# Fewer and wider warm-up matmuls, one matrix loaded in four parts, and two pairs of steps in another order, in a fused attention and mixture kernel

## The chip, the cores and the metric

The kernel runs on one core of one Trainium2 chip. The metric is the device time of one execution in microseconds (us); lower is better. Five engines work side by side, each through its own list of instructions: TensorE (PE in the profile; its weight loads are PEld), VectorE (DVE), ScalarE (ACT), GpSimd (POOL) and SyncE (SP). POOL and SP mostly issue DMA transfers here.

## What is computed

Two stages, the second fed by the first (from the reference, shortened):

```python
# q, k, v: 4 batches x 8 heads x 768 x 64;  sort_net: 4 x 8 x 8 x 8
for _ in range(5):
    P = exp(P - max(P));  P = P / sum(P, -1);  P = P / sum(P, -2)
k_sorted, v_sorted = P @ blocks_of(k), P @ blocks_of(v)     # 8 blocks of 96 rows are mixed
attn = softmax(q_blk @ k_sorted_blk.T / 8)                  # inside each block
x = (attn @ v_sorted_blk), heads side by side               # 3072 x 512
out = sum over 4 experts of p[:, e] * (relu(x @ w1[e]) @ w2[e])   # w1: 512 x 1024, w2: 1024 x 512
```

## The kernel before

The whole order of work is written out by hand; no scheduler moves anything. It falls into three stretches.

**The head (0 to about 28 us).** DVE and ACT run the five normalisation rounds on a 32 x 64 tile (lines 283 to 299), a strict chain of small operations. PE has nothing real to do yet and runs dummy matmuls: `warm(84)` at line 280 and `warm(30)` at line 288, each a 128x128 stationary tile with 128 moving columns. Between the two it transposes the first half of batch 0's queries (`h_q`, line 264). When the weights of the mixing are ready, `r_half(0)` (line 314) spreads half of them into PSUM, `build_PI0` makes mixing matrices, and `mix_half` and `mixed` (lines 485 and 503) mix batch 0's keys and values for four of the eight blocks: the product on PE, the evacuation from PSUM on ACT or DVE. `h_s` (scores and exponential), `h_w` (values transposed), `h_a` (attention times values), `h_x` (result transposed) follow for each quad of heads, interleaved with `group0`, the first expert's first layer (lines 1365 to 1417). Line 1370 spreads the other half of the weights (`r_half(1)`), after the first scores `h_s(0, 0)` and before the transposes of `h_w`; line 1372 copies all of them from PSUM to the tile `Rs`, on DVE. PSUM tiles come from two pools of two buffers each, `psM` and `psA`, handed out in turn, so a new tile waits until the last reader of the tile two before it is done. `mix_half("k", 1, 0, psm)` at line 1378 takes the buffer that line 1372 reads.

**The loads.** POOL issues the large loads in program order: queries, keys and values of batch 0, then `load_w1(0, 2)` (line 173), the first expert's first matrix in two parts of 256 rows each, and only then makes the masks (lines 175 to 204) and, at line 304, half of the spread weights (the other half is DVE's). Eight completion semaphores take turns, and a load waits until the load eight before it has landed. `group0` reads the matrix in the order: rows 0 to 255 with columns 0 to 511, rows 0 to 255 with columns 512 to 1023, then rows 256 to 511 in the same way.

**The middle (about 28 to 186 us) and the end.** The experts' products run chunk by chunk (`chunk`, line 809). Between two products stands a call of `slot()`, and a hand-written table, `PLANS`, says which attention step of the next batches runs in which slot: an entry `(c, n, f, b, pr)` runs step `f` for batch `b` and pair of heads `pr` in slot `n` of chunk `c`. `st_k` (line 392) mixes keys on PE and evacuates with four ACT copies (line 408); `st_v` (line 361) mixes values on PE, evacuates with one ACT copy (line 371) and, for every second pair, issues six DMAs on SP that move the values to `vs` (line 379); `st_s` is scores and exponential (line 425), `st_a` attention times values (lines 453, 434, 435). In slot 8 of batch 1's chunk 1 the second table, `PLAN_A`, also begins `input_sums`: an ACT multiplication (line 997) followed by a DMA that adds (line 998). After slot 9, `chunk` copies the product of bank A with ACT (line 856), and DVE adds bank B to that copy (line 857):

```python
            times(bankB, blk(1, 0), "b21", es)
            slot()
            nc.scalar.copy(p1[:], bankA)
            tt(oa1, bankB, p1[:], ALU.add)
            times(bankQ, sm(0), "t1", es)
            nc.scalar.copy(p5[:], bankQ)
            slot()
            ...
            times(bankA, sm(1), "t2", es, False)
```

Banks A and B are halves of one PSUM tile, and the product `t2` goes into bank A again. From 186 us on the remaining products run without attention steps.

Of the kernel before, what the change touches and what calls it, by code (L numbers as in the profile page):

```python
# [17 lines left out]
def kernel(  # L18
# [11 lines left out]
    nc = tc.nc  # L30
# [8 lines left out]
    P = 128  # L39
# [10 lines left out]
    KH = NFC // 2  # L50
# [16 lines left out]
    def psa(shape, dtype, name):  # L67
        state["n"] += 1
        return psA.tile(shape, dtype, tag="ps", name=name)
# [36 lines left out]
    def load_natural(b, nm, qd):  # L106
        src = {"k": k, "v": v}[nm]
        t = arena[:, ds(("k", "v").index(nm) * 2 * NW + qd * NW, NW)].rearrange("p (h r d) -> p h r d", h=4, r=R)
        natural[(b, nm, qd)] = t
        nc.gpsimd.dma_start(  # L110
            t.rearrange("p h r d -> p h (r d)"),
            src[b, ds(4 * qd, 4)].rearrange("h (p r) d -> p h (r d)", r=R),
        )
# [12 lines left out]
    w1sb, w2sb = [], []  # L126
# [4 lines left out]
    def load_w1(e, parts=1):  # L131
        n = NKC // parts
        for i in range(parts):
            nc.gpsimd.dma_start(
                w1sb[e][:, ds(i * n, n)], moe_w1[e].rearrange("(kc p) f -> p kc f", p=P)[:, ds(i * n, n)]
            )
# [8 lines left out]
    def load_half_queries(hf):  # L145
        for qd in range(2):
            nc.gpsimd.dma_start(
                q0[ds(64 * qd, 64), hf].rearrange("p h r d -> p h (r d)"), half_queries(qd, hf)
            )

    dummy = Hflat[:, ds(2 * NFC * 2 * P, P)]
# [18 lines left out]
    load_natural(0, "v", 0)  # L170
    load_natural(0, "k", 1)
    load_natural(0, "v", 1)
    load_w1(0, 2)

    eye16 = const.tile([P, CP], F16, name="eye16")
    maskk = const.tile([P, P], F16, name="maskk")
# [13 lines left out]
    kTs, ETs, vs0s, wide = [], [], [], []  # L190
# [38 lines left out]
    def spread_weights():  # L229

        nc.vector.tensor_reduce(p_den, p_in, AX.X, ALU.add)
        yield
        nc.vector.tensor_scalar(out=p_den, in0=p_den, scalar1=1e-9, scalar2=None, op0=ALU.add)
        yield
        nc.vector.reciprocal(p_den, p_den)
        yield
        nc.vector.tensor_tensor(
            p_out.rearrange("p e t -> p t e"), p_in, p_den.broadcast_to([P, NT, E]), ALU.mult
        )
        p_rows = p_dram.rearrange("e (p t) -> p e t", t=NT)  # L240
        nc.sync.dma_start(p_rows[0:S_P], p_out[0:S_P])
        nc.sync.dma_start(p_0, p_dram[0, 0:S].rearrange("(t p) -> t p", p=P))
        pbs[(0, 0)] = load_p(0, 0)
        nc.sync.dma_start(p_rows[S_P:P], p_out[S_P:P])
        yield
# [7 lines left out]
    qTs = {}  # L253
    q_ring = const.tile([P, 3, R, P], F16, name="q_ring")

    def warm(n):
        ps = psM.tile([P, 4, P], F32, tag="ps", name=f"ps_w_{state['n']}")
        state["n"] += 1
        for m in range(n):
            nc.tensor.matmul(ps[:, m % 4, :], dummy, dummy, start=True, stop=True)  # L260

    qT0 = [from_spare(2 * S).rearrange("p (s f r x) -> p s f r x", s=2, f=2, r=R) for _ in range(2)]

    def h_q(qd, hf, copy):

        ps = psa([P, 2, R, 64], F16, f"ps_q_{qd}_{hf}")
        rows = ds(64 * qd, 64)
        for sg in range(2):
            for r in range(R):
                for hh in range(2):  # L270
                    nc.tensor.transpose(
                        ps[ds(D * hh, D), sg, r, :], q0[rows, hf, 2 * sg + hh, r, :], ident[rows, rows]
                    )
        copy(qT0[qd][:, :, hf], ps[:])
# [2 lines left out]
    srow = const.tile([GH, NB, 1], F32, name="srow")  # L277
    scol = const.tile([GH, NB, 1], F32, name="scol")
    sn16 = const.tile([GH, NB, NB, CP], F16, name="sn16")
    warm(84)  # L280
    p_steps = spread_weights()
    nc.gpsimd.tensor_copy(ident6, ident[0:R, 0:R])
    for it in range(5):
        nc.scalar.activation(sn[:], sn[:], AF.Exp, bias=0.0, scale=1.0)
        if it == 4:
            for qd in range(2):
                h_q(qd, 0, nc.scalar.copy)
            warm(30)
        nc.vector.tensor_reduce(srow[:], sn[:], AX.X, ALU.add)
        nc.vector.reciprocal(srow[:], srow[:])  # L290
        nc.vector.tensor_tensor(sn[:], sn[:], srow[:].broadcast_to([GH, NB, NB]), ALU.mult)
        nc.vector.tensor_reduce(scol[:], sn[:].rearrange("p i j -> p j i"), AX.X, ALU.add)
        nc.vector.reciprocal(scol[:], scol[:])
        if it < 4:
            nc.vector.tensor_tensor(
                sn[:], sn[:],
                scol[:].rearrange("p j o -> p o j").broadcast_to([GH, NB, NB]),
                ALU.mult,
            )
            if it:  # L300
                next(p_steps)
# [10 lines left out]
    Rv = ps_R[:, :, 0:HB * GH].rearrange("p a (i g) -> p a i g", g=GH)  # L312

    def r_half(a):
        for i in range(HB):
            nc.tensor.matmul(
                Rv[:, a, i, :], sn16[:, a * HB + i, :, :].rearrange("g j c -> g (j c)"),
                ident[0:GH, 0:GH], start=True, stop=True,
            )
# [4 lines left out]
    Rs = const.tile([P, GH, NB], F16, name="Rs")  # L324
# [31 lines left out]
    vec, act = nc.vector.tensor_copy, nc.scalar.copy  # L356
# [128 lines left out]
    def mix_half(nm, qd, hf, pool, warm_up=0):  # L485

        ps = pool([P, 1024], F32, f"ps_m{nm}_{qd}_{hf}")
        keep_warm(ps[:, 0:P], warm_up)
        tails[(nm, qd, hf)] = ps[:, 2 * R * 64:1024].bitcast(F16).rearrange("p (n x) -> p n x", n=2)
        ps = ps[:, 0:2 * R * 64].rearrange("p (s r x) -> p s r x", s=2, r=R)  # L490
        for sg in range(2):
            for r in range(R):
                for hh in range(2):
                    h = 4 * qd + 2 * sg + hh
                    nc.tensor.matmul(  # L495
                        ps[ds(D * hh, D), sg, r, :],
                        head(0, nm, h)[:, r, :],
                        PI0[hf][:, h, :, :].rearrange("p i c -> p (i c)"),
                        start=True, stop=True,
                    )  # L500
        return ps

    def mixed(nm, qd, ps, i0, n, copy):

        dst = kTs[qd][:, 0:S] if nm == "k" else vT0[qd]
        copy(
            dst.rearrange("p (i x c) -> p x i c", i=HB, c=CP)[:, :, ds(i0, n)],
            ps.rearrange("p s r (i c) -> p (s r) i c", c=CP)[:, :, ds(i0, n)],
        )
# [30 lines left out]
    def h_s(qd, qq, ps=None):  # L540

        kT, ET = kTs[qd], ETs[2 * qd + qq % 2]
        if ps is None:
            ps = psa([P, 2, 512], F32, f"ps_s0_{qd}_{qq}")
        for n in range(4):
            for hh in range(2):
                sg, i = n // 2, 2 * (qq % 2) + n % 2

                m = BLK if 2 * i + sg == 3 else P
                nc.tensor.matmul(  # L550
                    ps[0:m, hh, ds(n * BLK, BLK)],
                    kT[ds(D * hh, D), ds((2 * i + sg) * BLK, m)],
                    qT0[qd][ds(D * hh, D), sg, qq // 2, :, ds((2 * (qq % 2) + n % 2) * CP, CP)],
                    start=True, stop=True,
                )
        nc.scalar.activation(
            ET[:, 0:S].rearrange("c (h x) -> c h x", h=2), ps[0:BLK, :, 0:HS],
            AF.Exp, bias=0.0, scale=SCALE,
        )
# [59 lines left out]
    def st_bk(b, qd):  # L619
# [24 lines left out]
            (0, 13, st_bv, 3, 1), (0, 14, st_a, 2, 3), (0, 14, st_x, 2, 2),  # L644
            (1, 0, st_k, 3, 0), (1, 1, st_v, 3, 1), (1, 1, st_x, 2, 3), (1, 1, st_q, 3, 2), (1, 2, st_s, 3, 0),
            (1, 3, st_k, 3, 1), (1, 4, st_v, 3, 2), (1, 4, st_q, 3, 3), (1, 4, st_bk, 3, 1), (1, 5, st_s, 3, 1),
            (1, 6, st_k, 3, 2), (1, 7, st_k, 3, 3), (1, 8, st_v, 3, 3), (1, 9, st_a, 3, 0), (1, 10, st_s, 3, 2),
            (1, 11, st_a, 3, 1), (1, 11, st_x, 3, 0), (1, 12, st_s, 3, 3), (1, 13, st_a, 3, 2), (1, 13, st_x, 3, 1),
            (1, 14, st_a, 3, 3), (2, 0, st_x, 3, 2), (2, 1, st_x, 3, 3),
        ],  # L650
# [715 lines left out]
    mixed("k", 0, mk0, 0, 2, act)  # L1366
    mv0 = mix_half("v", 0, 0, psa)
    mixed("v", 0, mv0, 0, 2, vec)
    h_s(0, 0)
    r_half(1)  # L1370
    mixed("k", 0, mk0, 2, 2, act)
    vec(Rs.rearrange("p g (a i) -> p a g i", a=2), Rv.rearrange("p a i g -> p a g i"))
    load_half_queries(1)
    load_w2(0, 2)
    build_PI0(nc.gpsimd, 1, 0, H, Rs[:, 0:H, HB:NB])
# [160 lines left out]
```

## Time and profile before

| | us |
|---|---|
| median of 3 runs | 359.47 |
| lowest and highest | 359.26, 360.56 |
| profiled execution, span from first to last instruction | 357.8 |
| PE busy in it | 351.6 (98%) |
| DVE, ACT, POOL busy | 276.2, 170.6, 133.6 |

The profile lists no other time for the profiled execution than its span, which lies 1.7 us under the median. How to read it: the page gives busy time by engine, the span in 40 slices, and the chain of work that ended last, followed back from the last instruction. Answers of the trace add, for any stretch, the instructions in order of time with the idle time ahead of each and what ended it (`[idle <-releaser]`), and the list of who waited for whom. By stretch, PE is busy for 9.96 of the first 12.00 us, 15.03 of the 16.00 us from 12 to 28, 131.99 of the 132.00 us from 28 to 160, 26.00 of the 26.00 us from 160 to 186, and 168.66 of the last 171.80 us. The granted clock reads 1.00 in all of these.

### The profile page before, as it was taken

The page shows a single profiled execution, that of the slowest core. Times are in us where ns is not written, and L with a number is a line of the kernel's source. Part 1 is how long each engine was busy: PE and PEld are TensorE (multiplying, and loading weights), DVE is VectorE, ACT ScalarE, POOL GpSimd, SP SyncE. Part 2 cuts the span into 40 slices and gives each one's busy share as a digit, 9 for nine tenths or more (in the row PEclk, how much of TensorE's full clock was granted, in tenths as well). Part 3 has the DMA queues.
Part 4 walks back from the last instruction along what each step waited for, and adds up shares of the span by engine and source line. Part 5 has one row for each costly group of instructions (what it writes and reads, how often), then busy time and mean ns, then how long its engine had stood idle before and what let it go on. Part 6 is the DMA issues. An engine that isn't in the chain of part 4 may idle for free.

```text
span 357.8 us, 9498 instructions
## 1 busy us (share of the span) xinstructions
PE 351.6 (98%) x3949; PEld 306.3 (86%) x3949; DVE 276.2 (77%) x552; ACT 170.6 (48%) x303; POOL 133.6 (37%) x149
## 2 busy tenths in 40 slices
PE   8899999999999999999999999999999999999996
PEld 8686867888888888888899988888888888888886
DVE  5754797869889587868978988896678886588963
ACT  2554240442434535367947258830288611688201
POOL 8864010375122222000535318840058800188400
PEclk9999999999999999999999999999999999999999
DMA  8999999999999999935996420005200015100011
GB/s 114 207 205 228 216 210 198 209 163 165 201 154 160 188 152 170 194 74 73 168 201 90 102 78 0 2 2 108 102 29 2 3 39 138 61 0 2 2 73 46
DMA packets 72022, 40.51 MB, mean 113 GB/s; under 512 B 40614, under 2 KB 66732, under 8 KB 71980
## 3 DMA queue, kind: packets, MB, share of 16 engines
q0 software_dynamic: 36576, 19.93, 41.9%
q1 hardware_dynamic: 35260, 19.92, 28.5%
q8 instruction: 31, 0.51, 0.6%
q14 instruction: 11, 0.09, 0.1%
q10 hardware_dynamic: 144, 0.07, 0.1%
HBM read 42.13 MB, written 6.34 MB: 135 GB/s over the span
## 4 chain that ended last, share of the span: by engine, by line
PE 95%; DVE 2%; ACT 1%; DMA 0%; issue 0%; DVEq 0%
PE ps_h L790 18%; PE ps_Q L1264 18%; PE ps_p L774 12%; PE ps_X L1121 10%; PE ps_Z L1121 7%; PE ps_Q L1121 7%; PE ps_Z L1264 6%; PE ps_h L679 3%; PE ps_o L714 3%; PE ps_p L830 3%; PE ps_a L453 2%; PE ps_s L418 2%; PE ps_k L399 1%; PE ps_v L365 1%; PE ps_a L567 1%; PE ps_mk L495 1%
## 5 line engine op out<-in xcount | busy, mean ns | idle before, releaser
L790 PE MATMUL ps_h<-xT,w 128*128 128x256 f16 x576 | 67.5, 273 | 0.0
L790 PEld LDWEIGHTS <-w 128*128 128x128 f16 x576 | 55.2, 98 | 7.2
L796 DVE SCALAR_TENSOR_TENSOR Hb<-ps_h,pb 128x1024 f16<-128x1024 f32 x34 | 41.5, 1223 | 17.2 <-PE ps_h L790 15.8
L1121 PEld LDWEIGHTS <-w 128*128 128x128 f16 x480 | 43.6, 98 | 4.8
L1134 POOL TENSOR_TENSOR arena<-tmp,pb 128x512 f16<-128x512 f32 x12 | 15.2, 1275 | 65.7 <-PE ps_Z L1121 49.8
L1264 PEld LDWEIGHTS <-Hb 128*128 128x128 f16 x320 | 31.1, 98 | 3.5
L1133 ACT ACTIVATE tmp<-tmp 128x512 f32<-128x512 f32 x46 | 29.0, 632 | 3.9 <-DVE tmp L1171 3.9
L1264 PEld LDWEIGHTS <-Sb 128*128 128x128 f16 x304 | 28.3, 98 | 3.0
L1121 PEld LDWEIGHTS <-arena 128*128 128x128 f16 x312 | 27.7, 98 | 2.9
L425 ACT ACTIVATE ET<-ps_s 96x768 f16<-96x768 f32 x24 | 18.0, 802 | 25.1 <-PE ps_s L418 24.8
L121 POOL DMA_DIRECT2D arena<-in_q_dram x24 | 19.9, 838 | 25.5 <-DMA q_ring<-arena 25.2
L408 ACT CAST kT<-ps_k 64x384 f16<-64x384 f32 x48 | 22.7, 473 | 13.3 <-PE ps_k L399 12.3
L1121 PE MATMUL ps_X<-ET,arena 128*128 128x256 f16 x168 | 25.2, 272 | 0.0
L1264 PE MATMUL ps_Q<-w,Hb 128*128 128x256 f16 x192 | 24.6, 273 | 0.0
L774 PEld LDWEIGHTS <-Hb 128*128 128x128 f16 x232 | 21.8, 98 | 3.0
L1127 DVE SCALAR_TENSOR_TENSOR Hb<-ps_X,pb 128x512 f16<-128x512 f32 x27 | 18.7, 691 | 7.0 <-PE ps_X L1121 7.0
L1141 ACT COPY ps_X<-ps_Z 128x512 f32<-128x512 f32 x27 | 15.4, 571 | 17.8 <-PE ps_Z L1121 17.8
L1121 PE MATMUL ps_Z<-xT,w 128*128 128x256 f16 (+1 forms) x176 | 22.5, 258 | 0.0
L760 DVE TENSOR_TENSOR Sb<-Hb 128x512 f16<-128x512 f16 x33 | 20.6, 647 | 0.0
L1148 ACT COPY tmp<-ps_X 128x512 f32<-128x512 f32 x26 | 15.2, 585 | 9.2 <-PE ps_X L1121 6.6
L1127 DVE SCALAR_TENSOR_TENSOR Hb<-ps_Z,pb 128x512 f16<-128x512 f32 x27 | 18.4, 682 | 1.3 <-PE ps_Z L1121 1.3
L1171 DVE TENSOR_TENSOR tmp<-ps_Q,tmp 128x512 f32<-128x512 f32 x26 | 17.8, 683 | 0.8 <-PE ps_Q L1121 0.8
(266 smaller groups left out, 741.6 us busy)
## 6 DMA issues: line engine op xcount, KB each, us to landing
w<-in_moe_w_dram POOLq DMA_DIRECT2D x6, 1024.0 KB, 27.9
pb<-p_dram SPq DMA_DIRECT2D x9, 512.0 KB, 7.0
arena<-in_k_dram POOLq DMA_DIRECT2D x8, 384.0 KB, 9.3
arena<-in_v_dram POOLq DMA_DIRECT2D x8, 384.0 KB, 7.5
vs<-arena SPq DMA_DIRECT2D x36, 66.0 KB, 4.9
arena<-in_q_dram POOLq DMA_DIRECT2D x24, 96.0 KB, 7.5
out_dram<-ob SPq DMA_DIRECT2D x9, 256.0 KB, 2.0
w<-in_moe_w_dram POOLq DMA_DIRECT2D x4, 512.0 KB, 12.5
```

What stands on the lines that cost most here:

```text
L121: nc.gpsimd.dma_start(t[:, h // 2, :, h % 2, :], q[b, h].rearrange("(t p) d -> p t d", p=P))
L408: nc.scalar.copy(kT[ds(D * hh, D), r], pk[ds(D * r, D), hh].rearrange("p a (i c) -> p a i c", c=CP),)
L425: nc.scalar.activation(ETs[2 * (pr % 2) + hh][:, 0:S].rearrange("c (a x) -> c a x", a=2), pss[hh][0:BLK, :, 0:HS], AF.Exp, bias=0.0, scale ...
L760: tt(sm[0], blk(0, 1), blk(1, 1), ALU.add)
L774: nc.tensor.matmul(ps, lhs(e, f), Ts[e][rhs][:, f, :], start=(first and e == es[0] and f == 0), stop=(done and e == es[-1] and f == KH - 1 ...
L790: nc.tensor.matmul(ps[:, f, :], w1sb[e][:, kc, ds((4 * g + f) * P, P)], xT[:, kc, ds(2 * c * P, 2 * P)], start=(kc == 0), stop=(kc == NKC ...
L796: nc.vector.scalar_tensor_tensor(out=Hb[:, homes.get(e, e), ds(4 * g, 4), :], in0=ps[:], scalar=0.0, op0=ALU.max, in1=weights(e).broadcast ...
L1121: nc.tensor.matmul(dst[:, ds(f * cols, cols)], a[lhs][:, k, ds((f0 + f) * P, P)], t[rhs][:, k, :], start=(first and f == 0 and k == 0), st ...
L1127: nc.vector.scalar_tensor_tensor(out=home(i, j), in0=src.rearrange("p (f x) -> p f x", f=m), scalar=0.0, op0=ALU.max, in1=weight(j).broadc ...
L1133: nc.scalar.activation(src, src, AF.Relu, bias=0.0, scale=1.0)
L1171: tt(t12, Q, u2, ALU.add)
L1264: nc.tensor.matmul(ps, lhs(e, f), Ts[e][rhs][:, f, part], start=(first and e == 0 and f == 0), stop=(e == E - 1 and f == KH - 1), skip_gro ...
```

## The change

Five edits:

1. The first matrix of the first expert is loaded in four parts (two halves of the rows, each in two halves of the columns) instead of two.
2. The first dummy sequence has 50 matmuls instead of 84; the second has 14 matmuls of 512 moving columns instead of 30 of 128.
3. `r_half(1)` moves ahead of `h_s(0, 0)`.
4. The copy to `Rs` moves with it, and from DVE to ACT.
5. In the table, `st_v` of batch 3's last pair of heads moves from slot 8 to slot 7 of chunk 1, and `st_k` of the same pair from slot 7 to slot 8.

```diff
-    load_w1(0, 2)
+    for i in range(2):
+        for j in range(2):
+            nc.gpsimd.dma_start(
+                w1sb[0][:, ds(2 * i, 2), ds(KH * P * j, KH * P)],
+                moe_w1[0].rearrange("(kc p) f -> p kc f", p=P)[:, ds(2 * i, 2), ds(KH * P * j, KH * P)],
+            )
...
-    def warm(n):
+    def warm(n, wide=1):
...
-            nc.tensor.matmul(ps[:, m % 4, :], dummy, dummy, start=True, stop=True)
+            nc.tensor.matmul(
+                ps[:, ds(m * wide % 4, wide), :],
+                dummy, dummy.rearrange("p (o x) -> p o x", o=1).broadcast_to([P, wide, P]), start=True, stop=True,
+            )
...
-    warm(84)
+    warm(50)
...
-            warm(30)
+            warm(14, 4)
...
-            (1, 6, st_k, 3, 2), (1, 7, st_k, 3, 3), (1, 8, st_v, 3, 3), (1, 9, st_a, 3, 0), (1, 10, st_s, 3, 2),
+            (1, 6, st_k, 3, 2), (1, 7, st_v, 3, 3), (1, 8, st_k, 3, 3), (1, 9, st_a, 3, 0), (1, 10, st_s, 3, 2),
...
     mixed("v", 0, mv0, 0, 2, vec)
+    r_half(1)
+    act(Rs.rearrange("p g (a i) -> p a g i", a=2), Rv.rearrange("p a i g -> p a g i"))
     h_s(0, 0)
-    r_half(1)
     mixed("k", 0, mk0, 2, 2, act)
-    vec(Rs.rearrange("p g (a i) -> p a g i", a=2), Rv.rearrange("p a i g -> p a g i"))
```

In the built program PE has 50 matmuls and 50 weight loads fewer, DVE one copy fewer, ACT one more, and POOL two DMAs more. In the middle ACT's order becomes: four copies of line 408 (pair 2), the copy of line 371, four copies of line 408 (pair 3), and then three multiplications of line 997; before, the copy of line 371 stood behind all eight. On SP the six DMAs of line 379 now stand ahead of the load of the next chunk's weights (line 217) and not behind it.

## The prediction

> **What bounds the kernel now.** The chain that ended last is PE's, and the list of PE's waits has six rows with 2.9 us between them:
>
> ```profile
> PE 95%; DVE 2%; ACT 1%; DMA 0%; issue 0%; DVEq 0%
> ```
>
> ```profile
> PE ps_w L260 <- DVE Hb L152: 1.1, 1, 1.1
> PE ps_R L316 <- DVE sn L304: 1.0, 1, 1.0
> PE ps_s L522 <- issue: 0.2, 1, 0.2
> PE ps_s L550 <- ACT kT L506: 0.2, 1, 0.2
> PE ps_s L550 <- issue: 0.2, 1, 0.2
> PE ps_mk L495 <- DVE Rs L1372: 0.2, 1, 0.2
> ```
>
> All six lie before 21 us. Up to 11.79 the bound is the DVE-ACT chain of the normalisation, which no edit touches; from there to 28 us it is the latency of PE, ACT and DVE handing to one another; from 28 to 186 PE is idle for 0.01 us. So time won in the head reaches the end, and any wait put into the middle is paid in full. I read the head as timeline, on PE and POOL:
>
> ```profile
> 8.97 1.85 PE L260 MATMUL ps_w<-Hb 128*128 128x128 f16 x30
> 11.79 0.26 PE L316 MATMUL ps_R<-ident,sn 32*128 32x32 f16 x4 [0.98 <-DVE sn L304]
> ...
> 14.17 0.33 PE L550 MATMUL ps_s<-Sb,kT 64*128 64x96 f16 x7 [0.18 <-issue]
> 14.44 0.26 PE L316 MATMUL ps_R<-ident,sn 32*128 32x32 f16 x4
> ...
> 15.21 0.57 PE L495 MATMUL ps_mk<-Sb,arena 128*64 128x64 f16 x24 [0.16 <-DVE Rs L1372]
> ```
>
> ```profile
> 6.25 1.43 POOL L134 DMA_DIRECT2D w<-in_moe_w_dram  x2
> ...
> 11.11 1.54 POOL L304 TENSOR_TENSOR sn<-sn,scol 32x512 f16<-32x512 f32 x1 [1.22 <-DVE scol L293]
> ```
>
> **Edit 2, dummies: 0.** Dummies start 107 ns apart until 5.99 us and 56 ns apart after, so the clock rises there. Fifty end at about 6.2 instead of 8.1. The query transposes (0.65 us from first to last) follow at 6.3, their data having landed by 5.88, and fourteen 512-column matmuls (starts 0.22 apart, as line 714's) take 3.0: PE ends near 10.2, not 10.7. Both lie before 11.79, where PE waits for DVE anyway. The pause grows from 1.2 to 1.6 us. No row shows a pause that costs the clock; if this one did, the 2.85 us of PE work from 11.79 to 15.20 would at worst double. I take 0, the rows with pauses of 1 us being nearest, and keep 2.9 as the far end. The Trainium skill, "TensorE: Matmul & The Clock Gate", section "What's actually happening", wants an idle window of about 3.4 us before the clock falls; by that the price is 0 too, and no run here shows it.
>
> **Edit 1, four parts: 0.** On POOL two issues of 0.72 more are 1.43; the 1.22 of idle ahead of line 304 takes most, and its product is ready at 12.9 instead of 12.65. In the transfer, packets of 2,048 bytes took 173 ns and packets of 1,024 took 98: 512 x 173 / 16 = 5.5 us becomes 1,024 x 98 / 16 = 6.3, so all behind lands 0.7 later. The nearest readers: the last part, landed at 21.18, now 21.9, is wanted at 22.0 (22.52 less the gain below); the second expert's neighbour matrix, landed at 39.67, now 40.4, is wanted at 42.3. The queue also waits for the load eight before: the second layer's first half now for keys landed at 13.87, which moves its issue by 0.3 us while over 5 us of transfers are queued. Nothing gains either: in the old kernel the halves landed at 18.01 and 21.18 and were first used at 19.19 and 21.68. 0 to 0.2; I take 0.
>
> **Edits 3 and 4: 0.5 gained by 24 us.** Now `r_half(1)` runs when the value mix has issued (13.40 + 0.13), ends by 13.8; its POOL half, ready at 12.9, is in time. ACT is free at 13.73, copies 128x256 in 0.37 (line 856's row), 13.83 to 14.2. The first scores still start at 13.78 (they wait for the cast that ends at 13.73). Before, this step had a stall of 0.39 from one matmul to the next (the row at 14.17); where it goes comes below. Without it they end at 14.1, and the exponential starts at 14.2, not 14.54. DVE loses its 0.42 copy: line 527 moves from 15.15 to 14.73, behind the transposes that wait for DVE's cast at 14.19. The third mix (15.21, waiting for `Rs`) starts at 14.55. Line 506's second value cast ends at 15.61, not 16.04. That last one releases the transposes at 16.09, from which the chain runs on to 19.85 with each wait on a thing that moved alike: 0.43. At 19.85 a second stall stood, 0.41 from one matmul to the next; without it the next step is released by DVE's line 581, also earlier, so 0.53 in all.
>
> **What takes part of it back: instruction blocks.** The two stalls lie 256 instructions apart in PE's list (before numbers 450 and 706). Packets of 16,384 bytes on the instruction queue start at 11.79, 17.86, 23.89 and 29.75, and the stalls end 1.45 after the first two have ended. So a block is fetched when PE enters the one before it (3.4 to 3.7 us later here), and is ready about 6.05 us after that. With 100 instructions fewer, block 450 is entered at 15.7 (ready by 14.2: no stall), block 706 at about 22.2 (ready by 21.8: none), and block 962, in the query transposes that stood at 28.35 and would now come at 27.8, is ready at 28.0 to 28.25. There PE stalls again. 0.1 to 0.35 is left of 0.53, or all if the block comes sooner; I take 0.25. By the Trainium skill, "Runtime: NRT & Kernel Launch", section "Instruction fetch mechanics", a block is 256 instructions and crossing into one costs a bump of a queue's tail, mostly hidden. This trace agrees on the size and disagrees on the hiding, by 0.39 and 0.41. By the page the whole 0.53 would stay.
>
> **Edit 5, the swap: 1.2 lost.** ACT at that place:
>
> ```profile
> 168.34 0.80 ACT L371 CAST arena<-ps_v 128x768 f16<-128x768 f32 x1
> 169.03 2.95 ACT L997 ACTIVATE arena<-w 128x1024 f16<-128x1024 f16 x3
> 171.88 0.36 ACT L856 COPY p<-ps_p 128x256 f32<-128x256 f32 x1
> ```
>
> ```profile
> 172.28 0.42 DVE L857 TENSOR_TENSOR oa<-ps_p,p 128x256 f32<-128x256 f32 x1
> ```
>
> ```profile
> 172.84 1.38 PE L774 MATMUL ps_p<-T,Sb 128*128 128x256 f16 x11
> ```
>
> ACT runs from 164.24 to 172.2 without a pause. `t2` on PE (172.84) goes into bank A's tile and waits for line 857, done at 172.71: slack 0.13. Now the single copy of `st_v` comes in slot 7 (ACT 166.25 to 167.05), and ACT then stands idle until PE has run `st_k` in slot 8 (167.8 to 168.1). Its four casts start 0.31 after PE's last, 168.39, and 0.50 apart: the last ends at 170.36. Behind them queue three of line 997 (0.95 apart), from 170.38 where they started at 169.03: 1.35 later. Line 856 ends at 173.6, line 857 at 174.05, and `t2` starts at 174.1: 1.25 late. `st_a`'s second head also waits, for the last cast (170.42 instead of 170.14), inside the same 1.25. Behind it all moves alike: DVE, the exponential (174.3), line 864 (177.0, wanted at 178.6). POOL's adding DMAs (line 998) wait for line 997 and go 1.3 later; their readers come after 186 and move too. On SP the six `vs` DMAs go 2 us earlier and the next chunk's weights (line 217) 4 us later, to about 171.3 plus 7.0 to land, wanted at 183.8. Nobody needs `vs` before 179, so nothing is won there. Bounds: 0, if ACT's order does not bind (the second rival), else 1.0 (the multiplications 0.2 closer together) to 1.35 (the whole ACT delay). I take 1.2.
>
> **The sum.** 0 + 0 - 0.25 + 1.2 = +0.95 on the span: 357.8 becomes 358.8. The median lies 1.7 over the span of the profiled execution; with that kept, 359.47 + 0.95 = **360.4 us**. With its bounds (-0.53 to -0.1, 0 to 0.2 for the parts, +1.0 to +1.35) this case alone spans 359.9 to 360.9.
>
> **Rivals.**
> - *The head keeps all.* Block 962 comes in time; by the waits of 14.17 and 20.27 it does not, but the fetch time is known only within 0.3. -0.53 + 1.2: 360.1.
> - *The swap is hidden.* For: PE had no wait at all there. Against: DVE's 1.0 us of idle behind ACT's line 856 in the list of waits, and the slack of 0.13. Then only the head counts: 359.2, at best 358.9.
> - *Slower outright: the clock falls in the longer pause* before 11.79. It decides if the pause of 1.6 us suffices for the throttle, or if its window falls badly. Price 1.5 (half of the 2.85 us of work sits on the chain) to 2.9, on top of +0.95: 361.9 to 363.3. Against: a pause of 1.2 kept it.
> - *It doesn't do what it says:* if the four parts were meant to end a wait for the matrix, there is none in PE's six rows.
>
> **Chances.** Forecast 0.47; head keeps all 0.16; swap hidden 0.16; clock falls 0.11; causes not named here 0.10 (0.04 faster, 0.06 slower by over 0.5%). Half a per cent, 1.8 us, is about what a measurement can tell from no change. The first three lie within it: 0.79 same; 0.11 + 0.06 = 0.17 slower; 0.04 faster. The range runs from the swap hidden (358.9) to the forecast with every bound against it (359.47 + 1.35 - 0.1 + 0.2 = 360.9), with the runs' scatter: 358.7 to 361.5, leaving out the fallen clock and the rest.
>
> **What would show it.** Right: a wait of PE for DVE's addition of banks A and B (line 865 now) of about 1.1 to 1.2 us near 173; ACT's three multiplications starting 1.3 later against the product `b11`; the pairs of gaps at 14.17 and 20.27 gone, and one of 0.2 to 0.5 in the query transposes near 28; the `Rs` copy on ACT at 13.8. Wrong: PE idle over 0.1 us anywhere else from 28 to 170, dummies or mixes at 107 ns apart after 11.79, a wait for the fourth part near 22, or no wait near 173.

## The result, and the profile after

The changed kernel takes 361.61 us (median of 6 runs, 360.74 to 362.09), the kernel before in the same session 359.51 us (6 runs, 359.26 to 360.56). The ratio is 1.0048, with a 95% interval of 1.0034 to 1.0062: slower by 1.2 to 2.2 us. The forecast was 360.4, so it fell 1.2 short, and the median lies 0.1 above the end of its range. The profiled execution is the quickest of the six: 360.74 us, span 359.0 us, against 357.8 before. The pair of profiles thus shows only half of what the medians show, and the other half had to be looked for in further profiles. Ratios, here and below, leave out runs that are over 1.5% above the fastest of the same kernel: four in experiment 1, one in experiment 6.

The list of PE's waits in the changed kernel (engine, line, what it waited for: total us, times, longest), and the page's line of the chain by engine:

```profile
PE ps_R L324 <- DVE sn L312: 1.7, 1, 1.7
PE ps_p L782 <- DVE oa L865: 1.2, 1, 1.2
PE ps_w L265 <- DVE Hb L152: 1.1, 1, 1.1
```

```profile
PE 92%; POOL 4%; ACT 1%; issue 1%; DVE 1%; POOLq 0%; ACTq 0%
```

The rows of the head that were 0.2 each are gone, the pause ahead of the sort matrix's transposes is 1.7 instead of 1.0, and one row is new: 1.2 us for DVE's addition of banks A and B. The timeline there, on ACT, DVE and PE (start, length, engine, line; in brackets the idle time before and what ended it):

```profile
167.94 1.97 ACT L416 CAST kT<-ps_k 64x384 f16<-64x384 f32 x4 [1.28 <-PE ps_k L407]
169.94 2.95 ACT L1005 ACTIVATE arena<-w 128x1024 f16<-128x1024 f16 x3
172.91 0.37 ACT L864 COPY p<-ps_p 128x256 f32<-128x256 f32 x1
```

```profile
173.32 0.42 DVE L865 TENSOR_TENSOR oa<-ps_p,p 128x256 f32<-128x256 f32 x1 [1.43 <-ACT p L864]
```

```profile
173.79 1.91 PE L782 MATMUL ps_p<-T,Sb 128*128 128x256 f16 x16 [1.23 <-DVE oa L865]
```

This is the chain that the prediction drew: idle ACT, four casts, three multiplications, the copy, the addition, PE. If each matmul of the two traces is set beside its counterpart, counted from the end, the changed kernel is 0.45 us ahead from 22 us to 168 us and 0.93 us behind from 175 us to the last matmul. The swap cost 1.38; the head gave 0.45. What comes after the last matmul took 0.18 longer, which makes 1.1 on the span.

A second profile of the changed kernel (361.68 us, span 359.9) shows a run near the median. Expected of it, before it ran, was the same head, the same wait near 173 and one more wait behind a landing, for `pb` near 97 or for POOL's adding DMAs near 190. PE's waits:

```profile
PE ps_R L324 <- DVE sn L312: 1.3, 1, 1.3
PE ps_p L782 <- DVE oa L865: 1.2, 1, 1.2
PE ps_w L265 <- DVE Hb L152: 1.1, 1, 1.1
PE ps_h L798 <- DVE Hb L804: 0.7, 1, 0.7
```

The fourth row is the missing part. It stands near 97 us, and DVE's timeline tells why; first this profile, then the first profile of the changed kernel, then the kernel before:

```profile
97.00 2.36 DVE L804 SCALAR_TENSOR_TENSOR Hb<-ps_h,pb 128x1024 f16<-128x1024 f32 x2 [2.31 <-DMA pb<-p_dram]
```

```profile
94.94 1.22 DVE L804 SCALAR_TENSOR_TENSOR Hb<-ps_h,pb 128x1024 f16<-128x1024 f32 x1 [0.25 <-PE ps_h L798]
```

```profile
96.39 2.53 DVE L796 SCALAR_TENSOR_TENSOR Hb<-ps_h,pb 128x1024 f16<-128x1024 f32 x2 [1.25 <-DMA pb<-p_dram]
```

DVE multiplies by `pb`, the probabilities of the chunk, and `pb`'s load landed at 96.90, 93.24 and 96.29. In the kernel before PE did not wait yet, but DVE already did. Matmul by matmul the second profile is 0.46 ahead until 97 us, 0.44 behind after it, 1.82 behind after 175: -0.46 for the head, +0.90 for `pb`, +1.38 for the swap, and 0.24 behind the last matmul. That is 2.06. It is the account of one run against one run, and it comes out at the difference of the medians (2.10) because both runs lie near the medians of their kernels.

### The profile page after: what moved, and what is told of

Read it like the earlier page. It is cut to its first block, busy times and chain, and to the rows that moved or that the text cites. A ratio compares the mean times of both kernels' runs of the same rounds, so it can differ in the third digit from the quotient of the medians.

```text
span 359.0 us, 9403 instructions
## 1 busy us (share of the span) xinstructions
PE 350.8 (98%) x3899; PEld 303.8 (85%) x3899; DVE 275.7 (77%) x551; ACT 170.9 (48%) x304; POOL 135.1 (38%) x151
## 4 chain that ended last, share of the span: by engine, by line
PE 92%; POOL 4%; ACT 1%; issue 1%; DVE 1%; POOLq 0%; ACTq 0%
PE ps_h L798 18%; PE ps_Q L1272 18%; PE ps_p L782 11%; PE ps_X L1129 10%; PE ps_Z L1129 7%; PE ps_Q L1129 7%; PE ps_Z L1272 6%; PE ps_o L722 3%; PE ps_h L687 3%; PE ps_p L838 3%; PE ps_a L461 2%; PE ps_s L426 1%; PE ps_k L407 1%; PE ps_v L373 1%; POOL arena L110 1%
## 5 line engine op out<-in xcount | busy, mean ns | idle before, releaser
L804 DVE SCALAR_TENSOR_TENSOR Hb<-ps_h,pb 128x1024 f16<-128x1024 f32 x34 | 41.5, 1223 | 17.3 <-PE ps_h L798 17.1
```

What stands on the lines that cost most here:

```text
L804: nc.vector.scalar_tensor_tensor(out=Hb[:, homes.get(e, e), ds(4 * g, 4), :], in0=ps[:], scalar=0.0, op0=ALU.max, in1=weights(e).broadcast ...
```

## The experiments

All twelve were compared with the kernel before on the same chip, but not all on one chip: experiments 1 (first run) to 4 share one, 5, 6 and the first of 7 another, the last stands on a third. Three of the twelve are single profiled runs: two of experiment 1, and the second profile above. Spans and granted clocks are known for every timed run, traces for one run of each.

**1. The swap alone.**

```
-(1, 7, st_k, 3, 3), (1, 8, st_v, 3, 3)
+(1, 7, st_v, 3, 3), (1, 8, st_k, 3, 3)
```

> The kernel before with edit 5 alone. If ACT's queue carries the cost (four late casts, behind them three multiplications, behind them the copy of the product b11), PE waits 1.3 to 1.4 us for DVE's addition near 173 us, and the time is 1.3 to 1.4 us over the kernel before, with the head as it was. If the wait in the changed kernel came from the head's new timing (every later stage arrives 0.45 us earlier, its transfers do not), the swap alone costs 0 to 0.9. If the runs of this kernel scatter up to 1.3 us above the fastest, as those of the changed kernel do, the scatter belongs to the swap.

Measured: the profiled run took 360.63 us (span 358.8), with this wait in line 774 and the same shift, from 0.47 ahead at 161 us to 0.92 behind at 180:

```profile
PE ps_p L774 <- DVE oa L857: 1.2, 1, 1.2
```

Two more profiles of this kernel follow (360.65 and 361.38 us), both with that wait. So the swap alone makes the wait; it needs nothing of the head. But the timed runs spread from 360.63 to 368.71 (median 364.68; ratio 1.0081, 1.0047 to 1.0116), and no run of the changed kernel did. Five of the twelve lie at 360.6 to 361.2, 1.1 to 1.6 over the kernel before, as the trace has it; the other seven lie at 363.65 or more. The head surprised too: it was 0.46 us ahead of the profile before, although it is the head of the kernel before.

> The kernel of edit 5 alone a second time, for another profile, since its runs spread from 360.6 to 368.7 us and the one profile shows the quickest. If the spread comes from POOL's adding DMAs (s3 of expert 3 lands late, n2 waits for it in POOL's queue, s4 for n2, and behind them stand POOL's own additions of line 1134, which had only 0.63 us of idle left in that profile), a run over 364 shows PE waiting for Hb of line 1134 or what follows it near 193 to 200 us, and the landing of the fourth adding DMA later than 185.1. If it comes from the load of pb issued at 170.5, DVE waits for that near 184 to 188. In a quick run: 360.6, as before.

> Edit 5 alone for a third profile: seven of its twelve timed runs lay above 363 us, both profiles so far were quick (360.6). If this one is slow, a second wait stands in it beside the 1.2 us near 173: behind POOL's adding DMAs near 190 to 200 (their chain s3, n2, s4 had 0.6 us to spare), behind pb near 184 to 188, or behind a transposing DMA. If it is quick, the place of the spread stays open.

Neither profile caught one of the long runs, so the place of the spread stays open. In the first, POOL had 0.63 us of idle ahead of its own additions, behind its chain of adding DMAs, where the kernel before had 2.15; that is a suspicion, not a finding.

**2. Edits 1 to 4, without the swap.**

```
-(1, 7, st_v, 3, 3), (1, 8, st_k, 3, 3)
+(1, 7, st_k, 3, 3), (1, 8, st_v, 3, 3)
```

> The changed kernel with the plan of before: edits 1 to 4. By the traces aligned matmul by matmul the head won 0.45 us by 22 us, so: 0.45 faster than before, span 357.4, no row of PE's waits near 173. If the head's gain is lost where the old plan has no slack either, the same time as before. If the part of the changed kernel's median that its profile does not show (about 0.9 us) comes from the head, the median here is near 359.9, above the kernel before, although the profiled span is below it.

Measured: 361.14 us, ratio 1.0044 (1.0031 to 1.0058). PE's waits:

```profile
PE ps_R L324 <- DVE sn L312: 1.5, 1, 1.5
PE ps_h L798 <- DVE Hb L804: 1.2, 1, 1.2
PE ps_w L265 <- DVE Hb L152: 1.1, 1, 1.1
```

The wait near 173 is gone, and the head is 0.46 ahead, but `pb` landed at 97.37 and PE lost 1.37 for it. Three of six runs had a mean clock of 0.995. So the four edits of the head, which by the prediction win 0.25 together, cost 1.6 by themselves. That is hardly less than all five cost (1.0048, and the intervals overlap): the price of the swap is read from the traces, and this pair of timed results doesn't show it.

**3. The swap kept, the three multiplications moved apart.**

```
-(1, 8, 2, 0), (1, 8, 2, 1), (1, 9, 3, 0), (1, 10, 3, 1)
+(1, 7, 2, 0), (1, 8, 2, 1), (1, 10, 3, 0), (1, 10, 3, 1)
```

> The changed kernel, the swap kept, but the three multiplications of the weights' sums that stood ahead of the copy of b11 are spread out: one goes to slot 7 (into ACT's idle 1.28 us ahead of the casts), one stays in slot 8, one goes to slot 10 behind that copy. If it is their place in ACT's queue that carries the cost, the wait of 1.2 us near 173 is gone and the time is that of the kernel without the swap: 1.4 us less than the changed kernel. If the late casts or the late value matrix themselves hold PE (its second head in line 461 waits for the last cast), 0.3 us or more of the wait stays. If SP's shifted transfers hold it, nothing changes.

Measured: the profiled run took 359.32 us (span 357.5). PE's waits, and ACT's timeline:

```profile
PE ps_R L324 <- DVE sn L312: 1.5, 1, 1.5
PE ps_w L265 <- DVE Hb L152: 1.1, 1, 1.1
```

```profile
166.65 1.06 ACT L1005 ACTIVATE arena<-w 128x1024 f16<-128x1024 f16 x1
168.04 1.96 ACT L416 CAST kT<-ps_k 64x384 f16<-64x384 f32 x4 [0.33 <-PE ps_k L407]
170.03 1.06 ACT L1005 ACTIVATE arena<-w 128x1024 f16<-128x1024 f16 x1
171.11 0.37 ACT L864 COPY p<-ps_p 128x256 f32<-128x256 f32 x1
```

The casts are as late as before (168.04), and the copy of `b11` stands at 171.11 instead of 172.91; the wait of 1.2 is gone. So late casts alone don't make PE wait, and neither do the three multiplications alone, which stood ahead of that copy in the kernel before too; it takes the three behind the late casts. SP's transfers are shifted here as in the changed kernel, so they are not it. Over nine runs the time spread from 359.32 to 363.33, median 361.49, 0.1 under the changed kernel, so that the 1.4 us are seen in the trace and not in the median; two of the nine had a clock of 0.995 or less.

**4. Edits 3 and 4 alone** (the second half of the sort matrix's transposes ahead of the first scores, its copy on ACT).

> The kernel before with edits 3 and 4 alone: 84 and 30 dummies, the matrix in two parts. If the stalls at 14.17 and 20.27 us are waits for instruction blocks at fixed numbers in PE's list, block 450 now begins inside the transposes of the second half of the sort matrix, which stall until 14.17 with the scores behind them: the head wins nothing (0 to 0.3 us slower than before). If the gain came from the reordering by itself, it is here too: 0.4 to 0.5 us faster than before.

Measured: 359.89 us, ratio 1.0011 (1.0002 to 1.0019): no gain. The expectation of a stall did not come true: this run's clock rose at 4.60 us, PE entered its instruction blocks earlier, and no stall at a block showed. The head was 0.46 ahead of the profile before by 22 us, but so was the unchanged head in two of the three profiles of the swap alone, to 0.01 us; in the third PE waited for the first matrix. The 0.45 doesn't need the edits; it is a matter of the run. Here the 0.46 was kept to the last matmul, and what comes after that took 3.89 us instead of 3.41, so that the span is 357.9 as before (357.8); in the fourteen profiles this tail takes 3.36 to 3.92.

**5. Edit 2 with and without edit 1; edit 1 alone.**

```
-    for i in range(2):
-        for j in range(2):
...
+    load_w1(0, 2)
```

> The changed kernel without the swap and with the matrix in two parts: edits 2 to 4. Edits 1 to 4 took 361.1, edits 3 and 4 alone 359.9. If edit 1 is what costs (512 packets of 2048 bytes become 1024 of 1024 bytes, about 0.75 us more of full DMA engines, and all that the saturated queue brings lands later), this takes 359.1 to 359.9, 1.2 or more below edits 1 to 4. If the dummies cost it, it takes 361 as with four parts.

> The kernel before with edit 1 alone. If edit 1 costs by DMA time, 360.3 to 361 (0.7 to 1.5 over the kernel before), with the loss in waits behind landings (pb near 97, adding DMAs near 190). By the prediction 0 to 0.2 over the kernel before.

The edit is shown on the changed kernel without the swap; the second kernel is the one before with the same lines the other way round. Measured: edits 2 to 4 took 360.98 us, ratio 1.0034 (1.0017 to 1.0051); edit 1 alone 359.56, ratio 1.0005 (0.9987 to 1.0022). The four parts cost nothing that can be measured. Edit 2, the only one that separates the first of these from experiment 4 (1.0011, 1.0002 to 1.0019), does cost, though the two intervals just touch. One thing that it can do is in the first of the two profiles (span 361.3): PE's longest wait, the page's clock row, and busy times by stretch with PE's granted clock ahead of the DMA share.

```profile
PE ps_R L319 <- DVE sn L307: 2.0, 1, 2.0
```

```profile
PEclk9699999999999999999999999999999999999999
```

```profile
8.41:11.83 3.42, 1.41 (x8) 0.45 (x7) 2.91 (x12) 1.62 (x3) 2.12 (x13) 1.00 1.30 199
11.83:18.66 6.83, 6.82 (x144) 5.83 (x144) 3.08 (x7) 3.50 (x7) 6.48 (x10) 0.50 1.19 209
```

The clock fell to half from 11.83 to 18.66 us. PE had paused from about 9.8 to 11.8, and reached the matmul that stands at 19.40 in a profile with a quick head (experiment 4) at 21.27: 1.87 us. Behind `pb`, which landed at 99.62, it then lost another 1.75. The same stretch of 3.41 us, counted in steps of 3.41 from the rise of the clock, in the changed kernel and, with the old dummies, in the second profile of the swap alone, the emptiest that a head with the old dummies shows:

```profile
9.03:12.44 3.41, 1.68 (x17) 0.89 (x15) 2.66 (x10) 1.62 (x3) 3.19 (x16) 1.00 1.30 197
```

```profile
10.63:14.04 3.41, 2.02 (x68) 1.77 (x68) 2.20 (x6) 1.02 (x2) 2.93 (x4) 1.00 1.29 195
```

PE busy 1.41 of 3.42 us (41%) lost the clock, 1.68 (49%) and 2.02 (59%) kept it. The pause in the last of these is as long as in the run that lost the clock:

```profile
PE ps_R L316 <- DVE sn L304: 2.0, 1, 2.0
```

So the length of the pause alone doesn't decide: 2.0 us lost the clock in one run and kept it in another. How busy the step is in which the pause falls fits all fourteen profiles (in the other thirteen no step of the head is under 49%), but only one of them shows a fall. Where the steps lie differs from run to run: the clock rose anywhere from 3.80 to 6.71 us. (Ahead of this rise the profile has no record of the clock and reads 1.00, though the dummies start 107 ns apart there.)

The fallen clock is not the whole cost of edit 2. Eight of the twelve runs of edits 2 to 4 have a mean clock of 0.998 or more; their median is 360.66, still 1.05 over the kernel before. For edits 3 and 4 alone the difference is 0.32. The three such runs of experiment 2 lie 1.57 over it.

**6. A longer second train of dummies.**

```
-            warm(14, 4)
+            warm(19, 4)
```

> Edits 1 to 4 with 19 matmuls of 512 columns in the second train instead of 14: 1.1 us more, so PE's pause ahead of the transposes of the sort matrix is about 0.7 us shorter than the 0.9 of the old kernel's long pauses, and ends near 11.8 all the same. If the clock falls because the pause takes most of one of the throttle's 3.41 us windows (7 of the 18 timed runs with 14 matmuls and no swap show 0.995 or less), no run here shows a clock under 0.998 and the slowest runs go: about 360.3, 0.8 less than edits 1 to 4. If the clock falls for another reason, the same share of runs shows it. The wait for pb near 97 stays in either case.

Measured, edits 1 to 4 with it: 360.58 us, ratio 1.0016 (1.0004 to 1.0029), outside the interval without it (1.0031 to 1.0058). A mean clock of 0.995 or less stands in 1 of its 12 runs (the longest, 365.69), against 7 of 18 with the short train (experiments 2 and 5), 2 of 9 in experiment 3 and none of 7 in the changed kernel. With the old dummies it is none of 24 in experiments 4 and 5, two of 24 in experiment 7, and one of 88 runs of the kernel before, but 4 of 12 in experiment 1, all four among its long runs. A mean clock doesn't tell where in the run the clock fell; only the profile of experiment 5 does. PE's waits in the profile with the longer train:

```profile
PE ps_q L279 <- DMA T<-in_q_dram: 0.8, 1, 0.8
PE ps_h L798 <- DVE Hb L804: 0.4, 1, 0.4
PE ps_R L324 <- DVE sn L312: 0.2, 1, 0.2
```

The pause ahead of the transposes is 0.2 us, and the wait behind `pb` remains, 0.4. The three runs of experiment 2 with a full clock lay 1.57 over the kernel before, and the eleven here lie 0.67 over it; so the gain of the longer train may not be the clock's alone, and what else it is stays open.

**7. `pb` from ACT's queue; and with edit 1.**

```
-        pbs[nxt] = load_p(*nxt)
+        pbs[nxt] = load_p(*nxt, nc.scalar if nxt == (0, 2) else None)
```

> Edits 3 and 4 alone, and the load of pb for the third chunk, which stood on SP behind a transposing DMA and six small ones, issued from ACT's queue instead (ACT is idle there from 81.7 to 87.9 us; the last reader of the old pb ends near 83.8). If the transfer of pb is what eats the head's gain (landings at 93.2 to 97.4 us, wanted at 95.9), the idle of DVE ahead of its product near 96 is gone, and the runs draw together near 359.1 to 359.4, under the kernel before (359.6) and under edits 3 and 4 without it (359.9). If the gain is lost elsewhere, 359.9 as without it; if pb lands late because the 16 DMA engines are full and not because of its place in the queue, the idle stays.

> Edits 1, 3 and 4 with the old dummies and the old plan, and pb for the third chunk from ACT's queue. The profile with pb ahead and two parts of the matrix shows no idle of DVE for pb, but PE waits 0.8 us for the halves of the matrix near 18.8 us. If the two waits are what the 0.45 us of the head turned into, both are gone here, the spans draw together near 357.0 to 357.5 and the time is 358.8 to 359.3: 0.4 to 0.8 under the kernel before. If the four parts end no wait (the prediction's reading of them), or if a third transfer is late as soon as these two are not, it takes 359.6 to 359.9, as the kernel before.

The edit is made to the kernel of experiment 4; the second kernel has the four parts of the matrix as well. Measured: 359.80 us, ratio 0.9998 (0.9982 to 1.0014), and 359.40 us, ratio 0.9995 (0.9976 to 1.0013). In both profiles DVE no longer waits for `pb` (idle 0.25, for PE). That doesn't show that its place in SP's queue had made it late: issued from ACT it landed at 94.22 and 94.15, and from SP's queue it landed at 93.2 to 95.5 in seven other profiles, those in which the transposing DMA ahead of it was quick, as that DMA was in both of these (4.5 and 5.4 us). And the runs of the first did not draw together (359.15 to 361.41): `pb` is not all that varies. In its profile another wait stands in the head, as it does in the third profile of the swap alone, whose row this is:

```profile
PE ps_h L679 <- DMA w<-in_moe_w_dram: 0.6, 2, 0.3
```

PE waits for the halves of the first matrix, which landed at 19.31 and 21.81 in that run. In the other five profiles with two parts the first half landed at 17.95 to 18.66 and nothing waited. With the four parts (first landing 17.33, last 21.46) the wait is not there, and the profile of the last experiment has no wait left but the two of the normalisation; it is 0.45 ahead from 22 us to the last matmul, span 357.4. Seven of its twelve runs have spans of 357.3 to 357.6. But eight of the seventeen runs of the kernel before beside it do too, and the medians, 0.3 us apart, can't be told from each other. So no version tried here beats the kernel before by an amount that can be measured.

## Why the prediction was right or wrong

- **Edit 5, "1.2 lost": right in mechanism, and nearly in size as the traces have it.** 1.38 measured, just over its upper bound of 1.35; the wait is there in all five profiles that have the swap and the old places of the multiplications, and gone when these are moved apart. The timed runs do not confirm the size: with and without the swap they read 1.0048 and 1.0044, and the swap alone reads 1.0081, with seven long runs that no trace explains.
- **Edits 3 and 4, "0.53 in all": wrong.** The step took the stalls at 14.17 and 20.27, which one profile showed, for a property of the kernel. They belong to that run: its instruction block was fetched at 11.8 us, in two profiles of the swap alone, with the head unchanged, at 10.5 and 10.3, and there that head is as fast as with the edits. Five profiles have the unchanged head, and only the one that the prediction read reached the first layer at 19.19 without a wait for the matrix; three reached it at 18.82 to 18.85, as the heads with the edits did. By themselves the edits cost 0.1 to 0.7 us.
- **"There PE stalls again" (block 962): wrong.** The block was fetched at 25.16 and came in time; the changed kernel kept its 0.45 to 97 us in the one profile and to 168 in the other. The first rival had this right, though the lead that was kept was the run's and not the edits'.
- **Edit 1, "0 to 0.2; I take 0": right** (1.0005). "All behind lands 0.7 later" isn't seen: the load for which the prediction put 40.4 in place of 39.67 landed at 39.85 with edit 1 alone and at 40.16 in the changed kernel, and at 39.5 to 40.7 in profiles with two parts, so that the runs differ by more than the edit. And "Nothing gains either" was drawn from one run, as was the last rival, that it ends no wait: in two of the seven profiles with two parts the halves landed late (19.3 and 19.5) and PE waited 0.6 and 0.8 us for them; in the seven with four parts the first landed at 17.1 to 17.4 and nothing waited. No gain in time could be measured from this.
- **Edit 2, "I take 0": wrong, by about 0.8 us** (1.0034 against 1.0011 without it; a longer train, 1.0016 against 1.0044, takes back about 1.0). The step said "No row shows a pause that costs the clock" and asked for the length of the pause; in the one fall that a trace shows, the share of PE in a step of 3.41 us fits and the length of the pause doesn't. The rival of the fallen clock had the price (1.5 to 2.9; measured 1.87) and gave 0.11; with the swap taken out, 7 of 18 runs have a mean clock of 0.995 or less. But by these medians the fallen clock is the smaller part of what edit 2 costs: the runs with a full clock are still 1.05 and 1.57 over the kernel before, and the profiles of both experiments show PE waiting behind `pb` (1.6 and 1.2). And it isn't what the result shows: none of the seven runs of the changed kernel itself has a mean clock under 1.0.
- **The term that was missing: `pb`, 0.9 in the second profile of the changed kernel.** The edits' effect on transfers was followed to the "nearest readers" of the weights and to no further load, and the middle was declared free of waits because PE had none from 28 to 186 us. DVE had one, 1.25 us behind `pb` at 96.39, in the trace of before; PE was then at the edge of waiting, and time won ahead of that edge can be lost at it. Sum of the terms as measured: -0.46 + 0.90 + 1.38 + 0.24 = 2.06.
- **The sum, "+0.95": near to the first pair of profiles (+1.1) in part by luck.** The swap's term was sized from the right chain; the head's -0.25 stands against -0.45 that the run gave and the edits did not, and the rest is 0.18 after the last matmul.

Of the six profiles with the new dummies, four show PE waiting behind `pb`; of the six with the old ones and `pb` on SP, none. Whether the dummies make `pb` late, and how, isn't settled: in the kernel before, with the old dummies, it landed at 96.29, only 0.4 ahead of the earliest of those four. The block of instructions fetched at 61.5 to 62.3 us with the old dummies is fetched at 68.0 to 68.5 with a hundred instructions fewer, and the first transposing transfer of `q_ring`, which lands at 70.2 to 71.2 otherwise, landed at 71.5 to 72.2 in five of those six; the sixth (70.4) speaks against it. That the runs of 359.8 to 360.3 in the result all had this wait is concluded from one profile.

## What to carry to other kernels

A stall or a slack of a few tenths in one profile may belong to that run: look at two or three profiles of the same kernel before a gain is built on it, and at the spread of the runs. Where PE shows no wait, read the waits of the engines that feed it: an engine that already waits for a transfer marks a place where time won earlier can be lost again. When work is moved to another slot on one engine, list what stands behind it in each queue up to the next thing that the bound engine needs; that is where the cost of this swap lay in the traces, and where spreading three instructions took the wait away. And compare the timed runs with the account from the traces: here a wait that vanished from a trace hardly moved the median.

## What the runs showed of the hardware

- The granted clock changes in steps of 3.41 us (in each of the fourteen profiles its changes lie a whole number of such steps apart), at places that differ from run to run. In the one fall that was traced, a step in which PE was 41% busy came before the loss, which lasted two steps; where every step of the head was 49% busy or more, the clock stayed. The Trainium skill, "TensorE: Matmul & The Clock Gate", section "What's actually happening", has the window free-running and 3413 ns long, and the trace of experiment 5 agrees (5.00, 11.83 and 18.66 us are two windows apart). It lets the clock fall after an idle window, and the section "HAM oscillation — how this bites in real kernels" warns of gaps over some 3.4 us. Here a pause of about 2.0 us did it, in a window that was not idle; the measurement decides.
- A transposing transfer on SP's queue (the third of `q_ring`, issued near 80 us) took 4.5 to 7.2 us where it was issued 0.73 us or more ahead of a load of 384 KB on POOL's queue, in nine profiles, and 8.3 to 8.9 us where it was issued 0.65 us ahead or later, in five. `pb`, which SP issues behind it and six small transfers (but for experiment 7), landed at 93.2 to 95.5 us in the first case and at 96.3 to 97.4 in the second (99.6 in the run whose clock fell). The two go together; that the order of the two issues is the cause was not tested.
